# Loading the first K in three pieces and one V in one, in a GQA decode block

## The chip, the cores and the metric

The kernel runs on one core of one Trainium2 chip. The metric is the device time of one execution in microseconds (us), lower is better. Before the change three runs took 184.36, 184.40 and 184.57 us, median 184.40 us. One more execution was recorded by the profiler; it took 184.38 us, and all lines of the profile below are from it.

## The reference

Grouped-query attention of a decode step against a cache, with both projections (bfloat16):

```python
B, Sq, D = 8, 4, 512
Hq, Hkv, Sk, Dh = 32, 8, 2048, 128
q = (x @ wq).reshape(B, Sq, Hq, Dh).transpose(0, 2, 1, 3)
k, v = repeat(k_cache, 4, axis=1), repeat(v_cache, 4, axis=1)   # [B, Hkv, Sk, Dh] -> Hq heads
p = softmax(q @ k^T * Dh ** -0.5)
out = (p @ v).transpose(0, 2, 1, 3).reshape(B, Sq, Hq * Dh) @ wo
```

There are few queries: `x` has 32 rows. The bytes are in the caches (two of 33.6 MB) and the two weights (4.2 MB each), and each is read once: 75.5 MB.

## The kernel before, in words

**Units and slots.** The work is cut into NU = 8 units. Each has a K block and a V block of 4 MiB, 32 KiB in each of the 128 partitions. Six units (1 to 6, `single(u)`) are one sequence each with all eight KV heads. Units 0 and 7 are halves of the last two sequences: half the heads of each, and the two sequences are called members (`b`, or `m` in the matmuls). A ring in SBUF has NR = 4 slots of such a size. The loads take the slots in a fixed order (lines 148 to 154): K0, wq, K1, V0, K2, V1, K3, V2, ..., K7, V6, V7, wo. Nearly all are issued from the SP queue, the ones for slots that are not free yet with a wait in front.

**How a block is loaded** (`load_kv`, lines 110 to 133). `whole` makes one DMA of 4 MiB; `by_member` makes two of 2 MiB, one for each half of the slot, in rows of 16 KiB; `by_half` makes two of 2 MiB that split the keys. K of a single unit goes as one DMA with rows of 32 KiB, unless it is listed in `split` (line 155), which has V0 to V4 and K7. The first K is issued by line 162 on two queues: member 0 from SP, member 1 from ACT. Behind it SP issues `x` (line 163), wq (line 137), K1, and V0 in two halves.

**What uses them.** A unit goes through these steps:
- `turn` (line 213): eight DVE transposes turn K into `kt`, four tiles t of two transposes i each. For unit 0, transpose (t, i) reads quarter t of member i's keys, so the order is: quarter 0 of member 0, quarter 0 of member 1, quarter 1 of member 0, quarter 1 of member 1. These first four are written ahead of everything else (lines 411 to 413).
- The query projection: `x` is transposed on TensorE (line 416), then 32 matmuls with wq (line 425), ACT casts (line 432), DVE transposes to `qT` (line 436), POOL builds `q_bd` (line 231). It is made once, after the first four turns.
- `scores` (line 251) on TensorE, the maximum (line 264) and the softmax's exponentials on ACT (line 291), DVE transposes of the weights (line 305), copies into a block diagonal (line 315).
- `values` (line 331): 64 matmuls a unit, one for each key of a partition; every one reads that key's V of both halves of the slot (`v[:, :, key, :]`).
- at the end `project` (line 403) multiplies with wo, which arrives in five DMAs of 2048, 1024, 640, 256 and 128 KiB (line 146).

**Order.** The order of each engine's instructions is written out by hand (`manual_schedule`); the loop of line 442 runs scores of unit u ahead of values of unit u-1, and `issue` at its end puts the loads of the next free slots on SP. K of unit u+2 waits for the turns of unit u, V of unit u+1 for the values of unit u-1. The completion of DMAs is counted on eight semaphores, taken in turn: the ninth DMA uses the first one's again.

Of the kernel before, what the change touches and what calls it, by code (L numbers as in the profile page):

```python
# [17 lines left out]
def kernel(  # L18
# [9 lines left out]
    nc = tc.nc  # L28
# [13 lines left out]
    NU = B * Hkv // (G * NB)  # L42
# [30 lines left out]
    ring = ring_pool.tile([128, NR, NB, C * Dh], BF16, name="ring")  # L73
# [14 lines left out]
    def single(u):  # L88
        return FIRST < u < LAST

    def half_of(u):
        return NG - 1 if u == LAST else 0
# [8 lines left out]
    def take(key):  # L101
        slot_of[key] = n_loads[0] % NR
        n_loads[0] += 1
        return slot_of[key]

    whole = [(0, 1)]
    by_half = [(0, 0.5), (0.5, 1)]
    by_member = None

    def load_kv(kind, u, parts, engines=(nc.sync,)):  # L110

        slot = take((kind, u))
        cache = k_cache if kind == "k" else v_cache
        n = C * Dh
        if not single(u):
            rows = cache[NS1:, G * half_of(u) : G * half_of(u) + G].rearrange(
                "b g (s c) d -> (g s) b (c d)", c=C
            )
        elif kind == "v":
            rows = cache[u - 1].rearrange("(b g) (s c) d -> (g s) b (c d)", g=G, c=C)  # L120
        else:
            rows = cache[u - 1].rearrange("h (s c) d -> (h s) (c d)", c=NS * C)
        if kind == "k" and single(u):
            pairs = [(ring[:, slot, :, :].rearrange("p b n -> p (b n)"), rows)]
        elif parts is by_member:
            pairs = [(ring[:, slot, b, :], rows[:, b]) for b in range(NB)]
        else:
            pairs = [
                (ring[:, slot, :, int(h0 * n) : int(h1 * n)], rows[:, :, int(h0 * n) : int(h1 * n)])
                for h0, h1 in parts  # L130
            ]
        for i, (to, of) in enumerate(pairs):
            engines[i % len(engines)].dma_start(to, of)

    def load_wq():
        slot = take("wq")
        nc.sync.dma_start(
            ring[:, slot, :, :].rearrange("p b n -> p (b n)"), wq.rearrange("(p r) n -> p (r n)", r=R)
        )

    def load_wo():
        slot = take("wo")
        for gg, cuts in ((0, (0, RW)), (1, (0, 8, 13, 15, RW))):
            rows = wo[gg * G * 512 : (gg + 1) * G * 512, :].rearrange("(p r) j -> p (r j)", r=RW)
            for r0, r1 in zip(cuts, cuts[1:]):
                nc.sync.dma_start(ring[:, slot, gg, r0 * D : r1 * D], rows[:, r0 * D : r1 * D])
# [5 lines left out]
            loads.append(("k", u + 2))  # L152
    loads.append("wo")
    loads.reverse()
    split = [("v", 0), ("v", 1), ("v", 2), ("v", 3), ("v", 4), ("k", NU - 1)]

    def issue(done):

        while loads and n_loads[0] < done + NR:
            what = loads.pop()  # L160
            if what == "k0":
                load_kv("k", 0, by_member, (nc.sync, nc.scalar))
                nc.sync.dma_start(x_sb[:, :], x.flatten_outer_dims())
            elif what == "wq":
                load_wq()
            elif what == "wo":
                load_wo()
            elif what in split:
                load_kv(*what, by_member)
            else:  # L170
                load_kv(*what, by_half if what == ("v", NU - 1) else whole)

    issue(0)

    make_identity(nc, ident[:])
# [266 lines left out]
    for u in range(NU + 1):  # L442
# [19 lines left out]
        if u >= 1:  # L462
# [7 lines left out]
            if u == NU:  # L470
                joined(u - 1)
        issue(2 + 2 * u)

    o_last = psum_o.tile([128, DH], FP32, tag="o", name="o_last")
# [40 lines left out]
```

## Time and profile before

| | |
|---|---|
| median of three runs | 184.40 us (184.36 to 184.57) |
| the profiled execution | 184.38 us |
| its span, first to last instruction | 182.5 us, so 1.9 us lie outside |
| busy, share of the span | PE 75%, DVE 71%, ACT 39%, POOL 22% |
| HBM read | 75.53 MB, 414 GB/s over the span |
| DMA packets | 4938; under 512 B 512, under 2 KB 704, under 8 KB 960 |
| queues | SP's queue (q1) 73.47 MB in 4784 packets; ACT's (q10) 2.10 MB in 144 |
| first K: SP's half, ACT's half | issued at 0.75 and 0.74, landed 12.2 and 12.4 us later |
| x | issued at 1.19 us, landed 12.1 us later |

In the profile, times count from the span's start. A group row gives the line, the engine, the operation and its tiles, the number of instructions, the busy time and the mean ns of one, and then how long the engine stood idle just before them and who ended that. The slices cut the span in 40 equal parts of 4.56 us; a 9 there means busy for 90% or more.

### The profile page before, as it was taken

How to read it: one execution, taken by the hardware profiler on the slowest of the kernel's cores; microseconds unless marked ns; L12 is line 12 of the kernel's file. 1: busy time of each engine (PE TensorE's matmuls, PEld its weight loads, DVE VectorE, ACT ScalarE, POOL GpSimd, SP SyncE). 2: the span in 40 equal slices, each digit the busy share in tenths (PEclk: the TensorE clock that was granted, in tenths of full speed). 3: DMA queues.
4: the chain of work that ended last, by engine and by line, in shares of the span. 5: the costliest groups of instructions: out<-in, count | busy, mean ns of one | idle time of the engine just before them, and what ended most of it. 6: DMA issues, size and time to landing. Idle time of an engine off the chain costs nothing.

```text
span 182.5 us, 2386 instructions
## 1 busy us (share of the span) xinstructions
PE 136.6 (75%) x924; PEld 83.3 (46%) x924; DVE 128.7 (71%) x161; ACT 70.3 (39%) x91; POOL 39.3 (22%) x110
## 2 busy tenths in 40 slices
PE   0000076940999999998999898989399977899993
PEld 0000022310348635843783485358234852388971
DVE  6518025738994999599689957995399559967340
ACT  2000020019604940990395079109900792063010
POOL 8800006006200700430080035004400220023000
PEclk9999999995589999999999999999969999999999
DMA  6999999999999998999999999999999999999991
GB/s 226 431 485 395 424 460 406 424 445 449 452 384 427 456 461 382 420 460 452 391 417 453 460 402 418 431 478 424 391 435 424 435 427 435 415 426 438 427 385 42
DMA packets 4938, 75.70 MB, mean 415 GB/s; under 512 B 512, under 2 KB 704, under 8 KB 960
## 3 DMA queue, kind: packets, MB, share of 16 engines
q1 hardware_dynamic: 4784, 73.47, 94.3%
q10 hardware_dynamic: 144, 2.10, 2.8%
q8 instruction: 7, 0.11, 0.2%
q14 instruction: 3, 0.02, 0.0%
HBM read 75.53 MB, written 0.03 MB: 414 GB/s over the span
## 4 chain that ended last, share of the span: by engine, by line
DMA 42%; DVE 23%; PE 22%; issue 4%; ACT 3%; POOL 2%; SPq 1%; ACTq 0%; DVEq 0%; POOLq 0%
DMA ring<-in_wo_dram 16%; PE s_ps L251 16%; DMA ring<-in_k_cache_dram 15%; DVE kt L213 14%; DMA ring<-in_wq_dram 12%; DVE stat L264 4%; PE o_ps L331 4%; ACT p_sb L291 3%; PE psq L425 2%; DVE pt L305 2%; DVE stat L322 1%; POOL p_bd L315 1%; POOL q_bd L231 1%; PE s_ps L403 1%; DVE stat L272 0%
## 5 line engine op out<-in xcount | busy, mean ns | idle before, releaser
L251 PE MATMUL s_ps<-kt,q_bd 128*128 128x512 bf16 x256 | 69.5, 409 | 20.0 <-POOL q_bd L231 9.9
L213 DVE STREAM_TRANSPOSE kt<-ring 128x1024 f32<-128x1024 f32 x64 | 73.9, 1210 | 14.2 <-DMA ring<-in_k_cache_dram 11.4
L331 PE MATMUL o_ps<-ring,p_bd 128*128 128x256 bf16 x512 | 57.2, 273 | 0.0
L251 PEld LDWEIGHTS <-q_bd 128*128 128x128 bf16 x256 | 25.3, 102 | 63.0 <-issue 26.6
L331 PEld LDWEIGHTS <-p_bd 128*128 128x128 bf16 x512 | 49.8, 98 | 6.0 <-issue 0.2
L315 ACT COPY p_bd<-pt 32x1024 bf16<-32x1024 bf16 x44 | 45.8, 1041 | 1.5 <-DVE pt L305 1.1
L291 ACT ACTIVATE p_sb<-s_ps,stat 128x1024 bf16<-128x1024 f32 x16 | 17.7, 1110 | 72.2 <-DVE stat L272 72.2
L315 POOL COPY p_bd<-pt 32x1024 bf16<-32x1024 bf16 x16 | 17.0, 1065 | 105.9 <-DVE pt L305 93.2
L264 DVE TENSOR_REDUCE stat<-s_ps 128x1 f32<-128x1024 f32 x16 | 19.3, 1208 | 3.4 <-PE s_ps L251 3.4
L305 DVE STREAM_TRANSPOSE pt<-p_sb 128x512 f32<-128x512 f32 x16 | 11.4, 712 | 14.0 <-ACT p_sb L291 14.0
L231 POOL COPY q_bd<-qT 32x64 bf16<-32x64 bf16 x64 | 13.1, 231 | 20.7 <-DVE qT L436 19.0
L425 PE MATMUL psq<-ring,xT_sb 128*32 128x512 bf16 x32 | 3.6, 630 | 9.1 <-DMA ring<-in_wq_dram 9.1
L416 PE MATMUL xtp<-ident,x_sb 32*128 32x32 bf16 x4 | 0.3, 195 | 13.3 <-DMA x_sb<-in_x_dram 13.3
L436 DVE STREAM_TRANSPOSE qT<-q_sb 128x64 f32<-128x64 f32 x8 | 1.2, 214 | 8.8 <-ACT q_sb L432 8.8
L177 DVE MEMSET p_bd<- 128x2048 uint32 x3 | 5.3, 1765 | 2.0 <-PEq L499 1.2
L322 DVE TENSOR_SCALAR stat<-of_b,stat 128x2 f32<-128x2 f32 x8 | 6.3, 793 | 0.3
L416 PEld LDWEIGHTS <-x_sb 32*128 32x128 bf16 x4 | 0.2, 117 | 13.3 <-DMA x_sb<-in_x_dram 13.3
L425 PEld LDWEIGHTS <-xT_sb 128*32 128x32 bf16 x32 | 1.3, 140 | 10.5 <-issue 10.1
L432 ACT CAST q_sb<-psq 128x512 bf16<-128x512 f32 x2 | 1.2, 586 | 11.8 <-PE psq L425 11.8
L375 PEld LDWEIGHTS <-perm 128*128 128x128 bf16 x56 | 3.8, 97 | 2.0 <-issue 0.5
L419 ACT COPY xT_sb<-xtp 128x128 bf16<-128x128 bf16 x1 | 0.3, 266 | 11.2 <-PE xtp L416 11.2
L343 ACT ACTIVATE o_sb<-o_ps,stat 128x128 bf16<-128x128 f32 x8 | 2.9, 368 | 4.1 <-PE o_ps L331 3.9
(30 smaller groups left out, 46.4 us busy)
## 6 DMA issues: line engine op xcount, KB each, us to landing
ring<-in_k_cache_dram SPq DMA_DIRECT2D x6, 4096.0 KB, 22.7
ring<-in_v_cache_dram SPq DMA_DIRECT2D x12, 2048.0 KB, 23.6
ring<-in_v_cache_dram SPq DMA_DIRECT2D x2, 4096.0 KB, 29.6
ring<-in_k_cache_dram SPq DMA_DIRECT2D x3, 2048.0 KB, 27.2
ring<-in_wq_dram SPq DMA_DIRECT2D x1, 4096.0 KB, 21.0
ring<-in_k_cache_dram ACTq DMA_DIRECT2D x1, 2048.0 KB, 12.4
ring<-in_wo_dram SPq DMA_DIRECT2D x1, 2048.0 KB, 25.9
ring<-in_wo_dram SPq DMA_DIRECT2D x1, 1024.0 KB, 28.2
```

The source lines that it names most:

```text
L177: nc.vector.memset(t[:, :, :, :, :], 0.0)
L213: nc.vector.transpose(out=out, in_=in_)
L231: nc.gpsimd.tensor_copy(out=qb[k * 32 : (k + 1) * 32, m, :, g, b, :].rearrange("w (j e) q -> w j e q", e=2), in_=qT[of * 32 : (of + 1) * 3 ...
L251: nc.tensor.matmul(s_ps[t // 2][:, t % 2, :], lhsT=q_bd[u % 2][:, m, 2 * j + e, :, :, :].rearrange("w g b q -> w (g b q)"), rhs=rhs, start ...
L264: nc.vector.tensor_reduce(out=stats[u][0][:, h : h + 1], in_=s_ps[h][:, :, :].rearrange("q t n -> q (t n)"), axis=AX, op=ALU.max, negate=True,
L291: nc.scalar.activation(out=out, in_=in_, func=EXP, bias=stats[u][1][:, :], scale=scale, accum_out=stats[u][2][:, h : h + 1],)
L305: nc.vector.transpose(out=pt[:, :, :, :].rearrange("s c q e -> s (c q e)").bitcast(FP32), in_=ps[u, h][:, :, :, :].rearrange("q c s e -> q ...
L315: copy(out=pb[rows, :, g, :, :], in_=pt[rows, :, :, :])
L322: nc.vector.tensor_scalar_mul(stats[u][3][:, :], of_b[:, :], stats[u][4][:, :])
L331: nc.tensor.matmul(o_pss[u][:, :, :], lhsT=pbs[u, h][:, i // 2, :, :, i % 2].rearrange("s g q -> s (g q)"), rhs=v[:, :, key_of(u, h, i // ...
L375: nc.tensor.matmul(o_pms[r // 2][:, r % 2, gg, :], lhsT=perm[:, r, w : w + 128], rhs=o_sbs[u][:, b, :], start=(u == 0 and r % 2 == 0 and g ...
L425: nc.tensor.matmul(psq[g * T : (g + 1) * T, :], lhsT=xT_sb[:, r, :], rhs=w[:, (g * NB + gg) * rep * Dh : (g * NB + gg + 1) * rep * Dh], st ...
```

## The change

The first K is issued by a new pattern `by_lot`: the first quarter of member 0's keys (rows of 4 KiB, 512 KiB in all) from SP, all of member 1 (rows of 16 KiB) from ACT as before, and the other three quarters of member 0 (rows of 12 KiB, 1.5 MiB) from SP. The engines alternate over the list, so SP issues the first and the third piece, one behind the other, ahead of `x`. V4 leaves `split` and is one DMA of 4 MiB in rows of 16 KiB. The number of DMAs stays the same, 32.

```diff
+    by_lot = "by lot"
...
+        elif parts is by_lot:
+            pairs = [(ring[:, slot, 0, : n // 4], rows[:, 0, : n // 4])]
+            pairs += [(ring[:, slot, 1, :], rows[:, 1])]
+            pairs += [(ring[:, slot, 0, n // 4 :], rows[:, 0, n // 4 :])]
...
-    split = [("v", 0), ("v", 1), ("v", 2), ("v", 3), ("v", 4), ("k", NU - 1)]
+    split = [("v", 0), ("v", 1), ("v", 2), ("v", 3), ("k", NU - 1)]
...
-                load_kv("k", 0, by_member, (nc.sync, nc.scalar))
+                load_kv("k", 0, by_lot, (nc.sync, nc.scalar))
```

## The prediction

> **What bounds the kernel now.** I read the page's slices first. PE is idle at the start and busy later, DVE has holes throughout, but the DMA row does not end: after the first slice all slices but one show 9, and the slices move 384 to 485 GB/s until the last.
>
> ```profile
> DMA  6999999999999998999999999999999999999991
> GB/s 226 431 485 395 424 460 406 424 445 449 452 384 427 456 461 382 420 460 452 391 417 453 460 402 418 431 478 424 391 435 424 435 427 435 415 426 438 427 385 42
> ```
>
> Second, the chain in order of time. It starts with wq and ends with wo, and both are transfers; wo alone is 29.10 us of waiting.
>
> ```profile
> 1.65 21.02 DMA ring<-in_wq_dram
> ...
> 103.21 27.30 DMA ring<-in_k_cache_dram
> ...
> 149.32 29.10 DMA ring<-in_wo_dram
> ```
>
> A piece of 640 KiB does not take 29 us. It was issued at 149.32 and stood behind V6, V7 and the earlier pieces of wo. The same in the middle: K6, issued at 103.21, landed 27.3 us later, and at the stream's 430 GB/s that is some 11.7 MB, nearly three slots. So each load is asked for long before its bytes can move, and the stream never runs dry. The tightest place is K2. It is issued at 35.01, and V0, ahead of it, lands at 42.1 (issued at 3.2, with 38.9 us to landing, the longest of the ring's): 7.1 us in hand. K2 itself lands at 51.7 (35.01 + 16.7), and 4.19 MB in these 9.6 us are 437 GB/s: no gap.
>
> So the span is: 1.7 us until the first bytes, a stream that lasts to the last piece of wo (issued at 151.4, 28.0 us to landing: 179.4), and a tail to 182.5. Only three things change the end: when the stream starts, how many us its bytes need, and the tail. Work on an engine counts only if it moves a load by over 7 us.
>
> Third, the waits and groups around the changed load.
>
> ```profile
> L213 DVE STREAM_TRANSPOSE kt<-ring 128x1024 f32<-128x1024 f32 x64 | 73.9, 1210 | 14.2 <-DMA ring<-in_k_cache_dram 11.4
> L425 PE MATMUL psq<-ring,xT_sb 128*32 128x512 bf16 x32 | 3.6, 630 | 9.1 <-DMA ring<-in_wq_dram 9.1
> L436 DVE STREAM_TRANSPOSE qT<-q_sb 128x64 f32<-128x64 f32 x8 | 1.2, 214 | 8.8 <-ACT q_sb L432 8.8
> ```
>
> The reader is to see two idle stretches of DVE. In the timeline its memsets and sums end at 7.49; it waits 5.48 us for K0 and makes the first four transposes from 12.97 to 17.59 (4.62 us). Then it stands idle for 7.69 us, until 25.29, because its next instruction (L436) needs the projection, and that needs wq, which lands at 22.68.
>
> **The change, part by part.**
>
> *The first transposes.* K0's two halves landed together (0.75 + 12.2 = 12.95 and 0.74 + 12.4 = 13.14), so the engines take rows of the two queues in turn: were SP's rows drained first, 2 MiB at 430 GB/s from 1.7 on would have landed near 7 us, and DVE, whose first transpose needs that half alone, would have begun there. With rows in turn, the eight rows of 4 KiB per DMA engine go beside ACT's eight rows of 16 KiB. First quarter and member 1 then land together, when all but 1.5 MiB of K0 has moved: 3.7 us (1.57 MB at 430 GB/s) before the end at 13.0, near 9.3. Two transposes run to 11.6, two more from 13.0 to 15.3 instead of 17.6. That is 2.3 us earlier into an idle stretch that then lasts 10.0 us in place of 7.7, up to the same 25.29. Worth 0; the cover is the wait for wq. Were DVE not waiting there, it would be worth at most these 2.3 us.
>
> *x and wq.* SP's issues take 0.38 to 0.53 us each, so the added one puts x, wq, K1 and V0 back by 0.4 us on SP. They stand in a queue whose head is busy to 13 us, and V0, last of them, would be issued by 4.1 us and moves after 32 us. Cost 0. Ahead of wq stand the same bytes, so it lands at 22.7 as before, and the chain behind it (projection, q_bd, scores 0, K2's issue at 35.01) stays.
>
> *Rows.* 128 rows of 16 KiB become 128 of 4 KiB and 128 of 12 KiB: eight more per engine. The nearest row for small ones is the end of wo. Its first piece lands at 174.35 (148.45 + 25.9), its last at 179.4; between lie 2048 KiB in rows of 8, 5, 2 and 1 KiB, in 5.05 us, which is 415 GB/s; over the whole span it is 414 GB/s. Below zero: 0, as shorter rows give no reason for a gain in rate. Above: if all of the difference between 430 and 415 GB/s in these 5.05 us (0.18 us) belonged to their 32 rows per engine, eight more cost 0.05 us. I take 0.02.
>
> By the Trainium skill (DMA: Bandwidth & Descriptors, "Anatomy of one DMA") a DMA costs about 2.0 us and then its bytes at 436 GB/s, and its rules ask for 1 MiB or more per transfer; the 512 KiB piece would lose 2 us, and V4 in one piece give 2 us back. The wo pieces above speak against both: four of them in 5.05 us leave no room for 8 us. That fit is of single transfers, and here the next one is already queued.
>
> *The start of the stream.* The first slice moved 226 GB/s x 4.56 us = 1.03 MB, which at 430 GB/s takes 2.4 us; the first bytes go at 1.7, so 0.45 us of the remaining 2.86 are lost while the stream gets going. This is the unknown: the first rows on each engine are now 4 KiB. If the loss belongs to the bytes or to the time, nothing changes; if it goes with rows, it can double (+0.45); if short first rows avoid it, it goes (-0.45). No row of this profile shows a start with short rows. I take 0, as the ACT queue's first rows, which share these microseconds, stay as they are and SP's DMA is issued at the same 0.75.
>
> *V4 in one.* Same rows, one issue less (0.4 us of SP, which waits tens of us). The nearest rows: V4 in halves landed at 120.85 (the second issued near 95.85, 25.0), K5 ahead of it at 111.1 (86.91 + 24.2): 9.7 us. V5 in one landed at 140.2 (111.72 + 28.5), K6 ahead of it at 130.5: 9.7 us. The first half of V4 lands now at 116.0, but each matmul of L331 reads both halves, and values 4 starts only at 121.92, behind scores 5. So 0; bounds -0.1 to +0.1 from the rounding of these landings.
>
> *Semaphores.* From K0's third piece to V4 every DMA uses the next semaphore of the eight; from K6 on all are as before. The waits this puts on SP name DMAs that landed long ago, as before: K3 waits for the third DMA ahead of wq to be done, V4 for V1 and V2. 0.
>
> Sum: 0 + 0 + 0.02 + 0 + 0 + 0 us, on 184.38. The profiled execution lies 0.02 below the median, so **184.4 us**.
>
> **Rivals.**
> - *The start gets cheaper.* For it: 0.45 us are there to win and whatever comes off the start comes off the end, as nothing else holds the stream. The limit is the end itself: PE waits only 0.34 us for the third piece of wo, but its own work also hangs on landings (K7's half at 150.1 starts the last turns), so it moves along. Against: the loss ends by 4.6 us, and half the rows in it are the unchanged 16 KiB of ACT. 183.95 if all goes.
> - *The start gets dearer (slower).* The mechanism: each engine loses time on each of its first rows and not on their bytes. In the 2.86 us an engine moved 66 KB, four rows of 16 KiB, and lost 0.45 us: 0.11 us a row. Now eight short rows are added per engine at just this place. If four of them pay as the first rows did, it is +0.45: 184.85. It decides from 3.4 added rows on (0.37 / 0.11); the 66 KB alone hold only some 2.6 added ones, +0.3, so it must go on a little longer. For it: the first slice alone is slow. Against: rows of 1 to 8 KiB at the end of wo show no such loss.
> - *DVE bounds the head.* Then 2.3 us go: 182.1. Against it stands the 7.69 us of idle time behind the four transposes.
> - *It doesn't do what it says*: the first quarter lands no earlier than 13 us. Then all is as before: 184.4.
>
> **How the numbers follow.** My forecast (no change, with the rival that gives the same time) gets 0.57; the cheaper start, far enough to count, 0.23; the dearer start 0.18; DVE's head 0.02. A difference under 0.2% (0.37 us) can hardly be told from none here: the three runs differ by 0.21 us. So faster 0.25, same 0.57, slower 0.18. The range takes in the start's bounds (-0.45, +0.45), V4's (-0.1, +0.1), the rows' +0.05 and the spread of runs: 183.8 to 184.9.
>
> **What would show it.** DVE's first transpose (L213) near 9.3 instead of 12.97, with a second wait for K0 between the second and the third; L436 still at 25.3; the first matmul of L425 at 22.7; 128 packets more, all under 8 KB (960 to 1088); K2 issued near 35.0; the last piece of wo landing at 179.4. Wrong would be: a first slice clearly over or under 226 GB/s with wq and wo moved by the same amount (the start), wq landing earlier but wo not (a gap in the stream behind), or two slices of DMA below 9 around V4.

## The result, and the profile after

The kernel after takes **185.31 us** (four runs, 185.27 to 185.37); its ratio to the kernel before is **1.0046 (95% interval 1.003 to 1.0062)**. That is slower, by 0.8 us (0.6 to 1.1 by the interval), and above the top of the predicted range (184.9). Part of the executions of either kernel are disturbed and take 4 to 12 us longer, so every time below is the median of the undisturbed ones, and "one run" means that only one was left.

The profiled execution took 185.37 us with a span of 183.4 us, 1.0 us over before's 184.38. The page's DMA slices and packets:

```profile
DMA  6999999999999999999999999999999999999991
GB/s 200 385 451 457 443 407 407 432 422 475 407 425 429 479 409 398 429 479 429 393 425 461 439 398 425 429 482 414 411 418 439 422 436 429 416 427 443 423 372 40
DMA packets 5066, 75.70 MB, mean 413 GB/s; under 512 B 512, under 2 KB 704, under 8 KB 1088
```

The stream still has no gap: 9 in every slice but the first and the last. But the first slice moved 200 GB/s in place of 226 and the second 385 in place of 431. In MB that is (26 + 46) x 4.56 us = 0.33, or 0.76 us at 430 GB/s. The 128 added packets are there.

The same three transfers in the chain in order of time (start, us, what):

```profile
2.10 21.45 DMA ring<-in_wq_dram
...
103.39 28.05 DMA ring<-in_k_cache_dram
...
150.26 29.12 DMA ring<-in_wo_dram
```

wq lands at 23.55 where it landed at 22.67: +0.88. The third piece of wo lands at 179.38 against 178.42: +0.96. So nearly all of the loss is made before wq lands, and the rest of the stream only carries it to the end. DVE in the timeline (start, busy us, engine, line, the idle time before):

```profile
9.39 2.39 DVE L219 STREAM_TRANSPOSE kt<-ring 128x1024 f32<-128x1024 f32 x2 [1.90 <-DMA ring<-in_k_cache_dram]
13.86 2.37 DVE L219 STREAM_TRANSPOSE kt<-ring 128x1024 f32<-128x1024 f32 x2 [2.08 <-DMA ring<-in_k_cache_dram]
26.15 0.62 DVE L442 STREAM_TRANSPOSE qT<-q_sb 128x64 f32<-128x64 f32 x4 [9.92 <-ACT q_sb L438]
```

Before, the same two places were:

```profile
12.97 4.62 DVE L213 STREAM_TRANSPOSE kt<-ring 128x1024 f32<-128x1024 f32 x4 [5.48 <-DMA ring<-in_k_cache_dram]
25.29 0.62 DVE L436 STREAM_TRANSPOSE qT<-q_sb 128x64 f32<-128x64 f32 x4 [7.69 <-ACT q_sb L432]
```

(L219 and L442 are before's L213 and L436.) The change does what it says: the first transposes start 3.6 us earlier, in two pairs. What they gain is idle time ahead of L442, 9.92 us of it, and L442 itself is 0.86 us later, with wq.

Where in the head? The table by stretches, for before and then for after (last columns: the DMA engines' busy share and GB/s):

```profile
1.70:4.60 2.90, 0.00 (x0) 0.00 (x0) 2.52 (x2) 0.75 (x1) 2.90 (x3) 1.00 1.04 367
4.60:9.10 4.50, 0.00 (x0) 0.00 (x0) 2.51 (x4) 0.00 (x0) 3.67 (x10) 1.00 1.00 430
```

```profile
1.70:4.60 2.90, 0.00 (x0) 0.00 (x0) 2.53 (x2) 0.75 (x1) 2.90 (x3) 1.00 0.96 319
4.60:9.10 4.50, 0.00 (x0) 0.00 (x0) 2.51 (x4) 0.00 (x0) 3.65 (x10) 1.00 0.99 380
```

The stream now starts worse (48 GB/s over 2.9 us, 0.32 us) and stays slow for as long as the 4 KiB rows last, to 9.1 us (50 GB/s over 4.5 us, 0.52 us), although the engines are busy in both: 0.99 of the time for 380 GB/s. The queues' lines of the stretch from 4.6 to 9.1 us show what got longer. Before:

```profile
q1 hardware_dynamic: 62, 1.02, 52.6%
q10 hardware_dynamic: 56, 0.92, 47.5%
```

After:

```profile
q10 hardware_dynamic: 87, 1.43, 83.2%
q1 hardware_dynamic: 83, 0.28, 15.9%
```

A line gives the queue's packets, their MB and their share of 16 engines' time over 4.5 us, that is of 72 us. A 16 KiB row of ACT's queue (q10) took 0.475 x 72 / 56 = 0.61 us before and 0.832 x 72 / 87 = 0.69 us after. So the unchanged long rows take longer, beside the short ones.

### The profile page after: what moved, and what is told of

Read it like the earlier page. It is cut to its first block, busy times and chain, and to the rows that moved or that the text cites. A ratio compares the mean times of both kernels' runs of the same rounds, so it can differ in the third digit from the quotient of the medians.

```text
span 183.4 us, 2387 instructions
## 1 busy us (share of the span) xinstructions
PE 136.0 (74%) x924; PEld 83.2 (45%) x924; DVE 128.8 (70%) x161; ACT 70.2 (38%) x91; POOL 39.1 (21%) x110
## 4 chain that ended last, share of the span: by engine, by line
DMA 43%; DVE 27%; PE 17%; issue 5%; ACT 3%; POOL 2%; SPq 1%; ACTq 0%; DVEq 0%; POOLq 0%
DVE kt L219 18%; DMA ring<-in_wo_dram 16%; DMA ring<-in_k_cache_dram 15%; DMA ring<-in_wq_dram 12%; PE s_ps L257 11%; DVE stat L270 4%; PE o_ps L337 4%; ACT p_sb L297 3%; PE psq L431 2%; DVE pt L311 2%; DVE stat L328 1%; POOL p_bd L321 1%; POOL q_bd L237 1%; PE s_ps L409 1%; DVE stat L278 0%
## 5 line engine op out<-in xcount | busy, mean ns | idle before, releaser
L257 PE MATMUL s_ps<-kt,q_bd 128*128 128x512 bf16 x256 | 68.8, 406 | 20.6 <-POOL q_bd L237 9.9
L219 DVE STREAM_TRANSPOSE kt<-ring 128x1024 f32<-128x1024 f32 x64 | 74.0, 1209 | 12.2 <-DMA ring<-in_k_cache_dram 10.5
L442 DVE STREAM_TRANSPOSE qT<-q_sb 128x64 f32<-128x64 f32 x8 | 1.2, 213 | 11.0 <-ACT q_sb L438 11.0
L409 PE MATMUL s_ps<-ring,oP 128*32 128x256 bf16 x32 | 4.3, 272 | 0.5 <-DMA ring<-in_wo_dram 0.5
```

Of the source, the lines that this page charges most:

```text
L219: nc.vector.transpose(out=out, in_=in_)
L257: nc.tensor.matmul(s_ps[t // 2][:, t % 2, :], lhsT=q_bd[u % 2][:, m, 2 * j + e, :, :, :].rearrange("w g b q -> w (g b q)"), rhs=rhs, start ...
L409: nc.tensor.matmul(out_ps[half], lhsT=oP[gg][:, r, :], rhs=w[:, r, half * DH : (half + 1) * DH], start=(gg == 0 and r == 0), stop=(gg == N ...
```

## The experiments

There are three theories at first. A: a short row that is taken in turn with a long one of the other queue costs time. B: the 4 KiB rows cost time by themselves, in any company. C: the loss comes from V4 in one DMA or from the shifted semaphores.

**Which part of the change (e1, e2).** The change is taken apart. e1 is after with V4 in two again, e2 is before with V4 in one:

```diff
-    split = [("v", 0), ("v", 1), ("v", 2), ("v", 3), ("v", 4), ("k", NU - 1)]
+    split = [("v", 0), ("v", 1), ("v", 2), ("v", 3), ("k", NU - 1)]
```

> The first K in its three pieces, V4 still in two (33 DMAs). Theory A (each 4 KiB row that a DMA engine takes in turn with a 16 KiB row of the other queue costs it some 0.11 us; eight per engine, 0.87 us by the time wq lands): 185.3 us, wq's landing at 23.5 as in the kernel after. Theory B (the 4 KiB rows lose that time by themselves, in any company): the same 185.3. Theory C (V4 in one, or the shifted semaphores): 184.4 to 184.6, wq's landing back at 22.7.

> V4 in one DMA, the first K as before (31 DMAs). Theories A and B: 184.4, no change, wq's landing at 22.7. Theory C: 185.2 or more.

e1: 185.42 us (one run), wq at 23.52. e2: 184.71 us, ratio 1.0006 (0.9995 to 1.0016). The loss is the first K's alone; V4 in one costs at most 0.3 us by e2's interval, and C falls.

**Mixed queues or the rows themselves (e3, e4).** e3 issues all three pieces from SP; e4 cuts both members and issues them side by side:

```diff
-                load_kv("k", 0, by_lot, (nc.sync, nc.scalar))
+                load_kv("k", 0, by_lot, (nc.sync,))
```

```diff
+            pairs = [(ring[:, slot, b, : n // 4], rows[:, b, : n // 4]) for b in range(NB)]
+            pairs += [(ring[:, slot, b, n // 4 :], rows[:, b, n // 4 :]) for b in range(NB)]
```

> The three pieces as in the kernel after, but all three from SP, so that no row is taken in turn with one of another queue. Theory A: the loss goes, wq lands near 22.7 and the time is 184.4 to 184.6. Theory B: the same eight 4 KiB rows per engine cost the same 0.87 us, wq near 23.5, 185.3. If only the first rows of the stream count (theory D: 0.28 us of the loss lie in the first slice): wq near 23.0, 184.7.

> First quarters of both members as 4 KiB rows (member 0 from SP, member 1 from ACT), then both rests as 12 KiB rows (SP, ACT); V3 goes in one DMA too, so that there are 32. Twice the short rows, but only rows of one length are taken in turn. Theory A (it is the mix of lengths): little loss, wq near 22.8, 184.4 to 184.7. Theory B (short rows by themselves): twice the loss, wq near 24.4, 186.1.

e3: 185.40 us, ratio 1.0044 (1.0028 to 1.0061). e4: 186.13 us (one run), twice the loss. A falls, and B stands so far. In e3 the stretches show the loss where the short rows now are, at the very start:

```profile
1.70:4.60 2.90, 0.00 (x0) 0.00 (x0) 2.52 (x2) 0.33 (x1) 2.90 (x3) 1.00 0.96 275
4.60:9.10 4.50, 0.00 (x0) 0.00 (x0) 3.66 (x5) 0.00 (x0) 3.65 (x10) 1.00 1.00 421
```

92 GB/s under before's 367 for 2.9 us are 0.62 us, and then the rate is nearly whole.

**Place, length or addresses (e6, e7, e8, e9).** e6 puts the 12 KiB rows first, e7 cuts at one half. e8 reads the 4 KiB rows from a stretch without gaps, e9 cuts K7 instead of K0:

```diff
-            pairs = [(ring[:, slot, 0, : n // 4], rows[:, 0, : n // 4])]
+            pairs = [(ring[:, slot, 0, : n // 4], k_cache[NS1, 0].rearrange("(p c) d -> p (c d)", p=128))]
```

```diff
-                load_kv(*what, by_member)
+                load_kv(*what, by_lot if what == ("k", NU - 1) else by_member)
```

> The kernel after with SP's two pieces in the other order: 12 KiB rows first, the 4 KiB rows last. Theory B1 (rows of 4 KiB at a pitch of 16 KiB read one quarter of the addresses, and the 16 engines meet there) and B3 (any 4 KiB row costs some 0.1 us over its bytes): the loss only moves, wq lands near 23.5, 185.3. Theory B2 (it is the first rows of the stream that pay): 184.5 to 184.7, wq near 22.8.

> The kernel after with the cut in the middle: rows of 8 KiB and again 8 KiB for member 0. B3 (a price per short row): eight rows more per engine, as after, 185.3 or a little less. B1 (which part of the addresses is read at a time): half of them instead of a quarter, so a loss of 0.3 us at most, 184.4 to 184.8. B2 (the first rows pay): about half of after's loss, 184.8 to 184.9.

> The kernel after, but the first piece's 4 KiB rows come from one stretch of 512 KiB without gaps (all keys of one head) instead of the first quarter of every 16 KiB; so the first quarter of member 0's keys is other data than the reference's. Same rows, same bytes, same order. B1: the loss goes, 184.4 to 184.7, wq near 22.8. B2 and B3: 185.3, wq near 23.5.

> The first K as before; K7, late in the stream and on SP alone, is loaded in the three pieces instead (V4 stays in one, 32 DMAs). B1 and B3: the loss comes with it, K7's last piece and wo land some 0.8 us later, 185.3, while wq lands at 22.7. B2 (only at the stream's start): 184.4 to 184.6.

e6 185.12, e7 184.69, e8 185.27 us (one run each; before on that chip 184.66); e9 185.07 us, ratio 1.0026 (1.0013 to 1.0039). So a cut in halves seems free, and the loss is not bound to the start of the stream: K7 pays 0.4 us too. e6 lies between its two forecasts. e8 speaks against the addresses by its time, but its stretch from 4.6 to 9.1 us moved 427 GB/s, not 380. It lost at the start (326 GB/s, before 367) and later, where its 12 KiB rows, still with gaps, were read (386 GB/s from 9.1 to 12.0, after 432). That left it open.

**The start once more (f1 to f4).** f1 and f2 put wq ahead of K0, with and without the cut; f3 and f4 repeat e8 and e9.

```diff
-    loads = ["k0", "wq", ("k", 1)]
+    loads = ["wq", "k0", ("k", 1)]
```

> wq is issued first and the first K behind it in the three pieces of the kernel after, all on SP. Theory S (the loss is made at the start of the stream: short rows at its head get going worse): with wq's 32 KiB rows at the head it goes, the rows of 4 KiB take 159 ns as in K7, and the time is that of its twin f2, 184.4 to 184.8. Theory P (the 4 KiB rows at a pitch of 16 KiB, as long as the 16 engines run in step, as they do in the first 50 us): rows of 4 KiB at some 250 ns here too, 0.6 to 0.8 us over f2.

> The twin of f1: wq first, then the first K in two halves of 16 KiB rows, all on SP, V4 in one. Both theories: the start of the stream costs the 0.7 to 0.8 us before 5 us that it costs in the kernel before, 184.4 to 184.8.

> e8 once more (4 KiB rows from one stretch without gaps; the first quarter of member 0's keys is other data than the reference's), since its one trace also shows 0.4 us of long rows between 9 and 14 us, where no 4 KiB row runs any more. If those are chance: 184.8 to 184.9, that is, the pitch makes 0.5 us of the loss. If the pitch is worth nothing: 185.3.

> e9 once more, for an undisturbed trace. Its rows of 4 KiB took 159 ns each and K7 9.87 us against 9.81 before, yet its time was 0.26% over the kernel before's. If K7's pieces make that, its last pieces land later against wq than in the kernel before; if it is the head of the stream, wq lands later than 22.7.

f1 185.23 us (one run), f2 184.88 us (1.0012, 1.0002 to 1.0021), f3 185.03 us (one run; before on that chip 184.67), f4 185.21 us (1.0026, 1.0016 to 1.0036). f1's 0.35 us over f2 and f3's 0.36 us over before lie between their forecasts, and f2 is just above its own. f4's trace shows K7's short rows at work. Stretch 138.4 to 142.0 us, where V5 ends and K7's first piece runs, before and f4:

```profile
138.40:142.00 3.60, 3.60 (x27) 2.06 (x26) 3.60 (x4) 0.00 (x0) 0.00 (x0) 1.00 1.02 432
```

```profile
138.40:142.00 3.60, 3.14 (x25) 1.92 (x24) 3.59 (x4) 0.00 (x0) 0.00 (x0) 1.00 1.02 390
```

42 GB/s over 3.6 us are 0.35 us of the 0.5 that f4 is slower. (f4's expectation takes from e9 that K7 needs only 0.06 us more than before; f4's trace shows this loss instead.) So the cut costs 0.4 to 0.5 us in K7, some 0.35 us behind wq (one run), and 0.8 us at the start of the stream.

**What of the cut (f5 to f8).** f5 cuts member 0 by partitions, all rows staying 16 KiB; f6 and f7 repeat e7 and e6; f8 cuts at an eighth.

```diff
-            pairs = [(ring[:, slot, 0, : n // 4], rows[:, 0, : n // 4])]
+            pairs = [(ring[:64, slot, 0, :], rows[:64, 0])]
...
-            pairs += [(ring[:, slot, 0, n // 4 :], rows[:, 0, n // 4 :])]
+            pairs += [(ring[64:, slot, 0, :], rows[64:, 0])]
```

> The same three DMAs, x and wq at the same places in the queue, but member 0 is cut by partitions (0 to 63, then 64 to 127), so that all its rows stay 16 KiB long. If the loss comes with one more DMA at the head or with SP's later issues: 185.3. If it comes with how the rows are cut: 184.4 to 184.8, wq near 22.7.

> e7 once more (member 0 in rows of 8 KiB and 8 KiB): its one undisturbed run, 184.69, says that this cut costs nothing, as many rows and DMAs as it adds. If a price per added row holds: 185.3. If the length of the short row or the part of the addresses that it reads counts: 184.6 to 184.9.

> e6 once more (12 KiB rows first, 4 KiB rows last): its one undisturbed run took 185.12. If the 4 KiB rows pay because they stand at the head of the stream: 184.6 to 184.8. If they pay at any place, as in K7 and behind wq, some 0.4 us: 185.0 to 185.2.

> The kernel after with an eighth in place of a quarter: rows of 2 KiB, then 14 KiB. If each short row has its price (eight rows, 0.1 us each): 185.3 again. If the loss goes with the bytes that are read in short rows: half of it, 184.9 to 185.0. If it grows as the rows get shorter: over 185.6.

f6: 184.56 us, ratio 1.0002 (0.9992 to 1.0012). It has after's three DMAs, after's order and after's eight added rows per engine, and loses nothing; its wq lands at 22.61:

```profile
2.10 20.51 DMA ring<-in_wq_dram
```

So neither the added DMA nor the number of rows is the cause. f7: 185.19 us (one run; before on that chip 184.49), slower like e6; the 4 KiB rows' place at the head isn't needed. f8: 184.91 us, 1.002 (1.001 to 1.003): 256 KiB in short rows lose 0.4 us, where 512 KiB lost 0.8. That speaks for a price by the bytes in short rows, but f8's trace is of the longest of its ten runs, 185.04 us, and has wq 0.70 us late, so the half rests on the medians. f5: 190.54 us, 1.0354 (1.0292 to 1.0416): no control at all, but a loss of its own of some 6 us, seven times as large.

**Gaps or lengths (g1, g2).** Both keep after's rows, DMAs and order, and change only where in HBM member 0's bytes lie. g1 reads both pieces from stretches without gaps; g2 reads the 4 KiB rows at a pitch of 20 KiB and the 12 KiB rows without gaps, as g1:

```diff
+            keys = k_cache[NS1].rearrange("h s d -> (h s) d")
+            rest = keys[4096:10240].rearrange("(p c) d -> p (c d)", p=128)
+            pairs = [(ring[:, slot, 0, : n // 4], keys[:2048].rearrange("(p c) d -> p (c d)", p=128))]
...
+            pairs += [(ring[:, slot, 0, n // 4 :], rest)]
```

```diff
+            pairs = [(ring[:, slot, 0, : n // 4], keys[:10240].rearrange("(p c) d -> p (c d)", p=128)[:, : n // 4])]
```

> The kernel after, but both of SP's pieces come from stretches without gaps (4 KiB rows from 512 KiB, 12 KiB rows from 1.5 MiB), so all of member 0's keys are other data than the reference's. The rows, bytes, DMAs and order are those of after. Theory G (what pays are rows that skip part of every 16 KiB in HBM; in e8 and f3 the 4 KiB rows without gaps ran at 159 ns and the 12 KiB rows with gaps were long instead): no long rows after 5 us, 184.5 to 184.8. Theory L (it is the lengths 4 and 12 KiB): 185.0 to 185.3.

> As g1, but the 4 KiB rows lie at a pitch of 20 KiB: they skip four fifths of their stretch, and their starts fall on all four quarters of 16 KiB in turn (again other keys for member 0). If the gap itself pays: long 16 KiB rows of ACT beside them between 4.5 and 9 us as in after, 185.1 to 185.4. If it is that all rows start on the same quarter: none, 184.5 to 184.8.

g1: **184.79 us, ratio 1.0008 (0.9997 to 1.0019)**; g2: 185.68 us, 1.0059 (1.0043 to 1.0075). g1 settles the main point against the lengths: rows of 4 and 12 KiB that leave nothing out cost nothing that can be measured (at most 0.35 us by the interval). Its wq lands 0.1 us after before's, at 22.77, and its lines for 4.6 to 9.1 us have ACT's rows back at 0.697 x 72 / 83 = 0.60 us:

```profile
2.12 20.65 DMA ring<-in_wq_dram
```

```profile
q10 hardware_dynamic: 83, 1.34, 69.7%
q1 hardware_dynamic: 98, 0.48, 25.4%
```

Its rate in the two stretches comes back only in part (before 367 and 430 GB/s), though wq is just 0.1 us late, so for losses this small the landings and the times are the better measure:

```profile
1.70:4.60 2.90, 0.00 (x0) 0.00 (x0) 2.52 (x2) 0.75 (x1) 2.90 (x3) 1.00 1.06 349
4.60:9.10 4.50, 0.00 (x0) 0.00 (x0) 2.83 (x5) 0.00 (x0) 3.66 (x10) 1.00 0.95 404
```

g2 is no more than half a confirmation, and its time lies above what either side of its expectation named. From 4.6 to 9.1 us it is as fast as before, as expected of rows that don't all start on the same quarter of 16 KiB; but its start is worse than after's:

```profile
1.70:4.60 2.90, 0.00 (x0) 0.00 (x0) 2.52 (x2) 0.76 (x1) 2.90 (x3) 1.00 0.89 266
4.60:9.10 4.50, 0.00 (x0) 0.00 (x0) 2.51 (x4) 0.00 (x0) 3.66 (x10) 1.00 1.01 430
```

No kernel here is faster than before; f6, which also brings the first quarter earlier, equals it.

## Why the prediction was wrong, point by point

- **What bounds the kernel: right.** The stream has no gap before or after, and what the head lost (0.88 us at wq) stands at the end (0.96 us at wo). Two small slips carry nothing: the slices go down to 382 GB/s and not 384, and the 0.18 us of wo's pieces are 0.17 (2.10 MB in 5.05 us).
- **The first transposes: worth 0 as said, though 9.3 was met in part by luck.** The first pair starts at 9.39, the second at 13.86 where 13.0 was forecast; the cover, DVE's wait for the projection, held (9.92 us). But the stream was already late by then, and first quarter and member 1 did not land together: the quarter landed at 9.35 (0.75 + 8.6) and member 1 at 10.5 (0.74 + 9.8). The second transpose didn't wait for it only because the first ran until then.
- **x, wq and SP's issues: the cost of the issues is 0 (f6)**, but "wq lands at 22.7 as before" was wrong by 0.88 us. The bytes ahead of wq were the same; the rate at which they came was not.
- **Rows: the step that failed.** It took 0.02 us, at most 0.05, from the short rows of wo. The term measured 0.8 us by the times and 0.88 us at wq's landing. The bound of 0.05 was no bound: it allowed for a price per row, while the runs show a price that goes with where the rows lie in HBM and not with their number (g1 has the same rows without gaps and f6 as many rows, and neither pays). About half of it sits on rows that the change doesn't touch: 87 rows of ACT's queue at 0.69 in place of 0.61 us are, by an estimate, 0.4 us on each of the 16 engines. What made wo's rows a bad measure stays open. They leave gaps too (8, 5, 2 and 1 KiB of every 16 KiB) and lost at most 0.17 us. In the trace of before the first and the last of the 16 engines land their parts of a piece of wo up to 2.0 us apart, those of K0's halves 0.74 us; but for K7's halves it is 1.9 us, and K7 pays when it is cut. So engines in step are not what decides it.
- **The fixed 2 us per DMA** that the Trainium skill (DMA: Bandwidth & Descriptors, "Anatomy of one DMA") would have charged was rightly set aside: f6 adds a DMA at the head, e2 removes V4's second, and both times stay within 0.2%. That section gives its fit for DMAs issued from GpSimd, which the prediction didn't say; the ones here are issued from SP.
- **The start of the stream: sized too small, and cut off too early.** The bounds were -0.45 and +0.45 us, with 0 taken. The first 2.9 us lost 0.32 us, inside the bound; the other 0.52 us came between 4.6 and 9.1 us, where the prediction held the loss to be over. The rival "the start gets dearer" had sign and place right and named 0.11 us for each added row; eight rows at that price are 0.88 us, the measured loss, but it let only four pay. Its mechanism was wrong all the same: g1 has those rows and doesn't pay, and K7, far from the start, does.
- **V4 in one and the semaphores: 0, right** (e2).
- **The chances.** "Slower" had 0.18. For it spoke, used for the start alone, that no row of the trace of before showed 4 KiB rows at the head; a bound from the nearest row was taken as a bound on the thing.

**What is shown and what isn't.** Shown: the loss comes from the first K's cut; rows with 4 and 12 KiB of every 16 KiB cost it, the same rows without gaps don't; 8 and 8 KiB don't, though they leave gaps as well; ACT's unchanged rows slow down beside the 4 KiB ones. Not shown: why. A gap alone is not enough (f6, wo's pieces), and a loss shows where only the 12 KiB rows have gaps (e8 0.6 us, f3 0.36 us, one run each), though in after the stretch of these rows ran at 432 GB/s. g1 also reads other places of the cache than after; that the gaps and not the places make the difference is the simpler reading, but no run parts the two. The Trainium skill (DMA: Bandwidth & Descriptors, "Latency and other measured facts") reports, for copies between HBM tensors, a rate that falls from 207 GB/s at a row pitch of 512 KiB to 103 at 4 MiB, and infers streams in step that meet on the same HBM channels. It states no loss at 16 KiB. Such meeting could fit that g2's odd pitch takes the loss away after 4.6 us, but not g2's bad start, so it stays an inference here too.

## What to carry to other kernels

- When the DMA stream sets the end, a load is not paid by its bytes alone: cutting a row so that a pass reads a part of each stretch of HBM and leaves the rest for later can slow the other queue's rows too (here 4 KiB of every 16, 0.8 us for a 2 MiB piece). Compare the rate (GB/s) and the landings behind it, not only the share of busy time, which stays at 0.99.
- If a first piece must come early, cut where it is free (halves here, f6) or give the piece a stretch of its own in HBM (g1); and ask first whether what waits for it is waiting for something else.
- A bound from a similar row binds only as far as one knows what makes the price. Here the small rows of wo were similar in length and in pitch, and lost at most 0.17 us where the new ones lost 0.8.

## What was not expected of the hardware

- Rows of 16 KiB for 64 partitions at a time (f5) cost some 6 us, with the bytes unchanged and as many DMAs as after: 190.54 us against 184.49 (1.0354, 1.0292 to 1.0416; five runs from 190.23 to 192.95). Its trace, of an execution of 193.15 us, shows where: its second to fourth slices move 236, 212 and 202 GB/s, before's 431, 485 and 395. Why it is about half was not looked into.
- A transfer's loss appears on other transfers: in after the long rows of the other queue went from 0.61 to 0.69 us.
- wq first and all on one queue (f2) is 0.2 us slower than two queues with K0 first (1.0012, 1.0002 to 1.0021). Whether the order or the one queue makes it was not separated.
